# Rebuilding the head of an attention and MLP kernel: token-major scores by half supergroups, and two TensorE jobs handed to DMA

## The chip, the cores and the metric

One core of a Trainium2 chip. The metric is the device time of one execution in microseconds (us), and the median of several executions stands for a kernel. The time of an execution is about 1.8 us longer than the span of its trace. "Granted clock" is the share of full speed that TensorE's throttle granted; a run's mean of 0.994 stands for some 7 us at half speed (in after_again's trace, mean 0.994, the half speed lasts from 25.52 to 32.35 us, 6.83 us). All runs compared here are fast (a run counts as slow when it is over 1.5% above the fastest of its kernel), unless a text says otherwise.

## The reference, cut to what matters

```python
def mab(q, kv):                       # attention, one head, 128 channels
    s = scale * (q @ kv.T)
    a = softmax(s)
    return a @ kv
for b in range(4):                    # batches of N = 12480 tokens
    h = mab(inducing, x[b])           # 32 inducing rows read all tokens of x
    attn = mab(x[b], h)               # the tokens read the 32 rows back
    g = attn @ w_in                   # 128 -> 2048
    g = max(g, 0) + alpha * min(g, 0)
    out[b] = g @ w_out                # 2048 -> 128
```

The first `mab` is a reduction over all tokens of a batch: nothing of the second can start before the last token of x was read. For batches 1 to 3 the kernel hides it under the work of the batch before. For batch 0 nothing is there to hide it under: that is the **head**. The rest is the **body**.

## The kernel before

Tokens come in supergroups of 2048 (six, plus a rest of 192), and a supergroup has four groups (q = 0 to 3). In the body a step is four "ring fills" (matmuls of the attention weights with `hW` into four PSUM banks), their eviction through relu by ScalarE and VectorE, and sixteen output matmuls; a group has four steps. (`hW` is h times `w_in`. The activation is computed as (1 - alpha) relu(g) + alpha g: relu's part goes through `W1`, which is `w_out` scaled by 1 - alpha, and the linear part through one 128x128 matrix A = `w_in` (alpha `w_out`). The "alpha copies" are the small instructions that bring alpha into place for this.) The attention weights stand in SBUF four times over ("replicas"), so that four matmuls run side by side in the array (the first four fills all start between 28.47 and 28.48 us).

The head of before, with cuts:

```python
    def a_xpose_pe(st, u):                      # x of supergroup u to channel-major
        for i in range(2):
            ...                                 # 8 transposes into one bank, then a copy
    def a_scores(st, u, by_dma=True):
        for q in range(NQ):                     # 32 rows x 512 tokens, four at once
            mm(ps[32 * q : 32 * q + 32, :], IT[:], st.xT[:, u, q, :])
        ...                                     # exp, with the sums by accum_out
    def e_xpose_pe(st, u): ...                  # exp back to token-major: 4 transposes, a copy
    def a_accum(st, u, into=None, first=False): ...   # pooling: 16 matmuls
    ...
    for i in range(n - 1):
        a_xpose_pe(st, order[i + 1])
        if i > 0:
            e_xpose_pe(st, order[i - 1])
        a_scores(st, order[i], by_dma=False)
        if 0 < i < n - 2:
            a_accum(st, order[i - 1], pool, i == 1)
    ...
    h_den(st)                                   # 1 / softmax sum, folded into `fr`
    w_inT(0)                                    # half of w_in transposed by TensorE
    a_accum(st, order[n - 1], pool)
    pin(nc.vector.tensor_copy(out=st.hacc[:], in_=pool))
    warm(6)                                     # filler transposes, results unused
    h_transpose(st)
    warm(6)
    b_scores_pe(st, 0, 0)                       # replicas of group 0: scores + exp
    h_weights(st, first=True)                   # hW
    warm(8)
    # the body; tasks that ride in its first groups:
    for q in range(1, NQ):
        at(0, lambda q=q: b_scores_pe(st, 0, q), q, (240, "A", 480))
    at(0, lambda: w_inT(KC // 2), 3, (460, "A", 960))
    ...                                         # four sets of denominators, A = w_in W
```

The softmax here doesn't subtract the row's maximum and nothing guards it: scores larger than these inputs give would overflow.

Of the kernel before, what the change touches and what calls it, by code (L numbers as in the profile page):

```python
# [24 lines left out]
def kernel(  # L25
# [49 lines left out]
    gt_pool = ctx.enter_context(tc.tile_pool(name="gtp", bufs=4))  # L75
    rep_pool = ctx.enter_context(tc.tile_pool(name="repp", bufs=3))
# [23 lines left out]
    def new_batch(b):  # L100
        st = Batch()
        st.b = b
        st.xT = xt_pool.tile([C, NS, NQ, GRP], bf16, name="xT", tag="xT")
        st.xTr = xt_pool.tile([C, JR, PR], bf16, name="xTr", tag="xTr")
        st.xn = {}
        st.e1 = {}
        st.e1T = {}
        st.es = work.tile([P, NS + 1], f32, name="es", tag="es")
        st.hacc = work.tile([P, C], f32, name="hacc", tag="hacc")
        st.e2 = {}  # L110
        st.d = {}
        st.rep = {}
        st.rden = {}
        nc.vector.memset(st.es[:], 0.0)
        nc.vector.memset(st.hacc[:], 0.0)
        return st
# [32 lines left out]
    def a_xpose_pe(st, u):  # L149
        xn = st.xn[u]  # L150
        if u < NS:
            for i in range(2):
                tp = bank()[:].bitcast(bf16)
                for k in range(2 * NB):
                    q, j = 2 * i + k // NB, k % NB
                    pin(nc.tensor.transpose(
                        tp[:, k * P : (k + 1) * P], xn[:, q, j * C : (j + 1) * C], ident[:]
                    ))
                dst = st.xT[:, u, 2 * i : 2 * i + 2, :].rearrange("c q t -> c (q t)")
                if i == 0 or u == order[-1]:  # L160
                    pin(nc.vector.tensor_copy(out=dst, in_=tp))
                else:
                    pin(nc.scalar.copy(out=dst, in_=tp))
        else:
            tp = bank()[:].bitcast(bf16)
            for j in range(JR):
                pin(nc.tensor.transpose(
                    tp[:, j * PR : (j + 1) * PR], xn[:, j, :], ident[:PR, :PR]
                ))
            pin(nc.vector.tensor_copy(  # L170
                out=st.xTr[:].rearrange("c j p -> c (j p)"), in_=tp[:, :REM]
            ))

    def e_xpose_pe(st, u):
        e1 = st.e1.pop(u)
        tp = bank()[:].bitcast(bf16)
        if u < NS:
            e1T = work.tile([P, NB, P], bf16, name="e1T", tag="e1T")
            for j in range(NB):
                pin(nc.tensor.transpose(  # L180
                    tp[:, j * P : (j + 1) * P], e1[:, j * P : (j + 1) * P], ident[:]
                ))
            pin(nc.vector.tensor_copy(
                out=e1T[:].rearrange("p j m -> p (j m)"), in_=tp[:, : NB * P]
            ))
        else:
            e1T = work.tile([P, JR, M], bf16, name="e1Tr", tag="e1Tr")
            for j in range(JR):
                pin(nc.tensor.transpose(
                    tp[:PR, j * M : (j + 1) * M], e1[:, j, :PR], ident[:M, :M]  # L190
                ))
            pin(nc.vector.tensor_copy(
                out=e1T[:PR].rearrange("p j m -> p (j m)"), in_=tp[:PR, : JR * M]
            ))
        st.e1T[u] = e1T

    def a_scores(st, u, by_dma=True):
        ps = bank()
        if u < NS:
# [6 lines left out]
            if by_dma:  # L206
                e1T = work.tile([P, NB, P], bf16, name="e1T", tag="e1T")
                pin(nc.sync.dma_start_transpose(out=e1T[:], in_=e1[:]))
        else:
            mm(ps[0:M, :REM], IT[:], st.xTr[:].rearrange("c j p -> c (j p)"))  # L210
            e1 = e1r
            pin(nc.scalar.activation(
                out=e1[:, :, :PR],
# [3 lines left out]
            if by_dma:  # L217
                e1T = work.tile([P, JR, M], bf16, name="e1Tr", tag="e1Tr")
                pin(nc.sync.dma_start_transpose(
                    out=e1T[:], in_=e1[:].rearrange("m j p -> m (j p)")  # L220
                ))
        if by_dma:
            st.e1T[u] = e1T
        else:
            st.e1[u] = e1



    def a_accum(st, u, into=None, first=False):
        xn = st.xn.pop(u)  # L230
        e1T = st.e1T.pop(u)
        alone = into is None
        ps = bank() if alone else into
        if u < NS:
            for j in range(NB):
                for q in range(NQ):
# [4 lines left out]
                        start=(j == 0 and (alone or first)), stop=(j == NB - 1),  # L241
                        skip_group_check=not alone,
                    )
            if alone:
                pin(nc.vector.tensor_tensor(
                    out=st.hacc[:], in0=ps[:, :C], in1=st.hacc[:], op=ADD
                ))
        else:
            for j in range(JR):
                mm(  # L250
                    ps[0:M, :C], e1T[:PR, j, :], xn[:, j, :],
                    start=(j == 0 and alone), stop=(j == JR - 1),
                    skip_group_check=not alone,
                )
            if alone:
                pin(nc.vector.tensor_tensor(
                    out=st.hacc[0:M, :], in0=ps[0:M, :C], in1=st.hacc[0:M, :], op=ADD
                ))
# [22 lines left out]
    def h_weights(st, first=False):  # L281
# [8 lines left out]
        for j0, j1 in ((0, 1), (1, NJ)) if first else ((0, NJ),):  # L290
            pin(nc.vector.tensor_copy(
                out=st.hW[:, j0:j1, :].rearrange("m j k -> m (j k)"),
                in_=ps[:, j0 * P : j1 * P],
            ))

    def h_linear(st):
# [3 lines left out]
        pin(nc.vector.tensor_copy(out=st.hA[:], in_=pa[:, :C]))  # L300


    def b_scores(st, s):
        ps = bank()
        if s < NS:
# [3 lines left out]
            pin(nc.scalar.activation(out=e2[:], in_=ps[:], func=EXP, scale=scale))  # L309
            w = GRP  # L310
        else:
            mm(ps[0:M, :REM], st.hT, st.xTr[:].rearrange("c j p -> c (j p)"))
            e2 = work.tile([M, REM], bf16, name="e2r", tag="e2r")
            pin(nc.scalar.activation(out=e2[:], in_=ps[0:M, :REM], func=EXP, scale=scale))
# [7 lines left out]
    def b_rep(st, s):  # L322
# [3 lines left out]
        for r in range(4):  # L326
            pin(nc.sync.dma_start(out=rep[32 * r : 32 * r + 32], in_=dv))
        for q in range(nq):
# [3 lines left out]
    def b_scores_pe(st, s, q):  # L332
        if q == 0:
            st.rep0 = rep_pool.tile([P, NQ, GRP], bf16, name="rep", tag="rep")
        ps = bank()
        mm(ps[:], st.hT4[:], st.xT[:, s, q, :])
        pin(nc.scalar.activation(out=st.rep0[:, q, :], in_=ps[:], func=EXP, scale=scale))
        st.rep[s * NQ + q] = st.rep0[:, q, :]

    def b_den_pe(st, s, q):  # L340
        if q == 0:
            st.rden[s] = work.tile([P, NB, NQ], f32, name="rd", tag="rd")
        e2 = st.rep[s * NQ + q] if q else st.rep0[:, 0, :]
        ps = bank()
        for j in range(NB):
            mm(ps[:, j : j + 1], e2[:, j * P : (j + 1) * P], pick[:, 0:1])
        pin(nc.vector.reciprocal(
            out=st.rden[s][:, :, q : q + 1].rearrange("p j q -> p (j q)"), in_=ps[:, :NB]
        ))

# [134 lines left out]
    make_identity(nc, ident32[:])  # L485
    al_f = const.tile([KC, P], f32, name="al_f")
    nc.sync.dma_start(out=al_f[:], in_=moe_alpha.rearrange("(k p) -> k p", p=P))
    for u in order[3:]:
# [4 lines left out]
    pin(nc.gpsimd.dma_start(  # L493
        out=w_out_f[:], in_=moe_w_out.rearrange("(k p) c -> p k c", p=P)
    ))
# [5 lines left out]
    for q in range(4):  # L501
# [16 lines left out]
    alp = bank()  # L518
    alT = const.tile([P, KC], f32, name="alT")
    nc.tensor.transpose(alp[:, :KC], al_f[:], ident32[:KC, :KC])  # L520
    nc.vector.tensor_copy(out=alT[:], in_=alp[:, :KC])
    om_al = const.tile([P, KC], f32, name="om_al")
    nc.vector.tensor_scalar(
        out=om_al[:], in0=alT[:], scalar1=-1.0, scalar2=1.0, op0=MULT, op1=ADD
    )
# [4 lines left out]


# [9 lines left out]
    def warm(n):  # L541
        tp = accs[1][:].rearrange("p k c -> p (k c)").bitcast(bf16)
        for k in range(n):
            pin(nc.tensor.transpose(tp[:, k * P : (k + 1) * P], ident[:], ident[:]))

    def w_inT(k0):
        wtp = bank()[:].bitcast(bf16)
        for k in range(8):
            pin(nc.tensor.transpose(
                wtp[:, k * P : (k + 1) * P],  # L550
                w_in_b[:, (k0 + k) * P : (k0 + k + 1) * P], ident[:],
            ))
        pin(nc.scalar.copy(
            out=winT[:, k0 : k0 + 8, :].rearrange("p k c -> p (k c)"), in_=wtp
        ))
# [16 lines left out]
    pool = accs[0][:, 0, :]  # L572
    n = len(order)
    a_xpose_pe(st, order[0])
    for i in range(n - 1):
        a_xpose_pe(st, order[i + 1])
        if i > 0:
            e_xpose_pe(st, order[i - 1])
        a_scores(st, order[i], by_dma=False)
        if 0 < i < n - 2:  # L580
            a_accum(st, order[i - 1], pool, i == 1)
    a_scores(st, order[n - 1], by_dma=False)
    e_xpose_pe(st, order[n - 2])
    a_accum(st, order[n - 3], pool)
    h_sum(st)
    w_scale(W1, om_al)
    w_scale(AW, alT)
    e_xpose_pe(st, order[n - 1])
    a_accum(st, order[n - 2], pool)
    h_den(st)  # L590
    w_inT(0)
    a_accum(st, order[n - 1], pool)
    pin(nc.vector.tensor_copy(out=st.hacc[:], in_=pool))
    warm(6)
    h_transpose(st)
    warm(6)
    b_scores_pe(st, 0, 0)
    h_weights(st, first=True)
    warm(8)
# [15 lines left out]
    for q in range(1, NQ):  # L615
# [156 lines left out]
```

## Time and profile before

597.37 us, median of 3 runs (596.58 to 597.43). The trace below is of another, slower execution: its span of 597.17 us stands for a time of some 598.9 us (an estimate, with the 1.8 us of above).

| reading | us | view |
|---|---|---|
| last piece of x landed / w_in / w_out | 19.87 / 23.12 / 26.34 | landings of DMAs in the trace |
| last half's transposes begin | 21.38 | timeline |
| first ring fill | 28.47 | timeline |
| group 1's first fill | 35.20 | timeline |
| first output matmul of group 5 | 61.62 | timeline |
| end | 597.17 | trace |

From the page of before (busy times; then busy tenths in 40 slices of the span, and the granted clock in the same slices):

```profile
...
PE 582.9 (98%) x9186; PEld 435.0 (73%) x9186; DVE 518.6 (87%) x878; ACT 507.1 (85%) x994; POOL 84.9 (14%) x170
...
PE   4999999999999999999999999999999999999997
...
PEclk9999999999999999999999999999999999999999
...
```

TensorE is busy 98% of the span. Of the forty slices (14.9 us each) only the first and the last show less than nine tenths, and the body begins at 28.47 us: what a change of the head can win lies in these first 30 us.

From the timeline of before (start, duration, engine, line, instruction, count; in brackets the idle time before it and what ended it):

```profile
...
20.92 0.62 PE L156 MATMUL ring_85<-ident,xn 128*128 128x128 bf16 x8
...
21.38 0.61 PE L156 MATMUL ring_86<-ident,xn 128*128 128x128 bf16 x8
...
26.39 0.49 PE L94 MATMUL ring_82<-fr,hacc 128*128 128x128 f32 x2
...
27.26 0.39 PE L94 MATMUL ring_83<-xT,hT_494 128*128 128x512 bf16 x1
...
28.47 0.39 PE L94 MATMUL ring_85<-rep,hW 32*128 32x512 bf16 x1
...
30.24 1.05 PE L94 MATMUL acc_87<-W_168,gt 128*128 128x128 bf16 x16
...
35.20 0.38 PE L94 MATMUL ring_82<-rep,hW 32*128 32x512 bf16 x1
...
```

After the last transposes come scores, exp and pooling, then the transpose of the pooled rows (26.39), the replica's scores (27.26) and the first fill (28.47). Between them stand waits for copies and exps of the other engines, in part filled with the filler transposes: a chain, in which each piece stands behind the one before it.

### The profile page before, as it was taken

The page shows a single profiled execution, that of the slowest core. Times are in us where ns is not written, and L with a number is a line of the kernel's source. Part 1 is how long each engine was busy: PE and PEld are TensorE (multiplying, and loading weights), DVE is VectorE, ACT ScalarE, POOL GpSimd, SP SyncE. Part 2 cuts the span into 40 slices and gives each one's busy share as a digit, 9 for nine tenths or more (in the row PEclk, how much of TensorE's full clock was granted, in tenths as well). Part 3 has the DMA queues.
Part 4 walks back from the last instruction along what each step waited for, and adds up shares of the span by engine and source line. Part 5 has one row for each costly group of instructions (what it writes and reads, how often), then busy time and mean ns, then how long its engine had stood idle before and what let it go on. Part 6 is the DMA issues. An engine that isn't in the chain of part 4 may idle for free.

```text
span 597.2 us, 21700 instructions
## 1 busy us (share of the span) xinstructions
PE 582.9 (98%) x9186; PEld 435.0 (73%) x9186; DVE 518.6 (87%) x878; ACT 507.1 (85%) x994; POOL 84.9 (14%) x170
## 2 busy tenths in 40 slices
PE   4999999999999999999999999999999999999997
PEld 3677777777777777677777777777777777777775
DVE  2588899889889998899998989988988898998995
ACT  3588888898889888888888988889888889989886
POOL 6331111010111111101011111101011101101100
PEclk9999999999999999999999999999999999999999
DMA  9644799862237669983134478986212221221211
GB/s 197 161 93 103 162 161 176 172 105 85 68 87 147 134 141 173 166 154 112 40 99 120 101 162 157 173 177 103 86 68 80 80 98 57 83 97 56 93 46 61
DMA packets 79009, 69.18 MB, mean 116 GB/s; under 512 B 53200, under 2 KB 68448, under 8 KB 78912
## 3 DMA queue, kind: packets, MB, share of 16 engines
q0 software_dynamic: 12720, 39.30, 26.4%
q1 hardware_dynamic: 66048, 27.97, 24.2%
q8 instruction: 72, 1.18, 0.9%
q10 hardware_dynamic: 144, 0.52, 0.3%
q14 instruction: 25, 0.20, 0.1%
HBM read 39.94 MB, written 28.62 MB: 115 GB/s over the span
## 4 chain that ended last, share of the span: by engine, by line
PE 58%; ACT 0%; DVE 0%; issue 0%
PE acc_88 L94 21%; PE acc_87 L94 21%; PE ring_85 L94 3%; PE ring_83 L94 3%; PE ring_84 L94 3%; PE ring_82 L94 3%; PE ring_81 L94 3%; PE ring_86 L94 3%; ACT gt L405 0%; DVE gt L407 0%; DVE ob L456 0%
## 5 line engine op out<-in xcount | busy, mean ns | idle before, releaser
L94 PEld LDWEIGHTS <-gt 128*128 128x128 bf16 x6272 | 352.4, 98 | 78.9 <-issue 75.9
L94 PE MATMUL acc_87<-W_168,gt 128*128 128x128 bf16 (+1 forms) x3136 | 209.0, 220 | 0.0
L94 PE MATMUL acc_88<-W_168,gt 128*128 128x128 bf16 (+1 forms) x3136 | 208.8, 220 | 0.0
L465 POOL DMA_DIRECT2D out_dram<-ob x99 | 53.7, 542 | 492.8 <-DVE ob L456 422.3
L405 ACT ACTIVATE gt<-ring_83 128x512 bf16<-128x512 f32 (+1 forms) x160 | 95.5, 597 | 10.9 <-ACT gt L405 5.4
L405 ACT ACTIVATE gt<-ring_81 128x512 bf16<-128x512 f32 (+1 forms) x159 | 95.0, 597 | 11.2 <-PE ring_84 L94 5.6
L94 PE MATMUL ring_82<-rep,hW 32*128 32x512 bf16 (+1 forms) x270 | 101.6, 379 | 0.0
L94 PE MATMUL ring_83<-rep,hW 32*128 32x512 bf16 (+1 forms) x270 | 101.1, 378 | 0.0
L94 PE MATMUL ring_85<-rep,hW 32*128 32x512 bf16 (+1 forms) x267 | 100.4, 379 | 0.3 <-ACT gt L405 0.3
L94 PE MATMUL ring_84<-rep,hW 32*128 32x512 bf16 (+1 forms) x266 | 99.6, 378 | 0.8 <-DVE gt L407 0.8
L94 PE MATMUL ring_86<-rep,hW 32*128 32x512 bf16 (+1 forms) x264 | 99.3, 379 | 0.0
L94 PE MATMUL ring_81<-rep,hW 32*128 32x512 bf16 (+1 forms) x263 | 98.9, 379 | 0.0
L405 ACT ACTIVATE gt<-ring_84 128x512 bf16<-128x512 f32 x147 | 88.2, 600 | 12.0 <-ACT gt L405 5.4
L405 ACT ACTIVATE gt<-ring_85 128x512 bf16<-128x512 f32 (+1 forms) x147 | 87.7, 596 | 11.8 <-PE ring_82 L94 5.3
L405 ACT ACTIVATE gt<-ring_86 128x512 bf16<-128x512 f32 (+1 forms) x143 | 85.6, 599 | 12.3 <-ACT gt L405 5.9
L405 ACT ACTIVATE gt<-ring_82 128x512 bf16<-128x512 f32 (+1 forms) x142 | 84.9, 598 | 12.1 <-PE ring_85 L94 4.4
L407 DVE TENSOR_SCALAR gt<-ring_82 128x512 bf16<-128x512 f32 (+1 forms) x123 | 84.2, 684 | 8.5 <-PE ring_84 L94 4.1
L407 DVE TENSOR_SCALAR gt<-ring_86 128x512 bf16<-128x512 f32 (+1 forms) x116 | 79.4, 684 | 12.9 <-PE ring_82 L94 8.4
L407 DVE TENSOR_SCALAR gt<-ring_84 128x512 bf16<-128x512 f32 (+1 forms) x113 | 77.1, 682 | 9.3 <-PE ring_85 L94 3.8
L407 DVE TENSOR_SCALAR gt<-ring_85 128x512 bf16<-128x512 f32 x115 | 78.9, 686 | 7.1 <-PE ring_81 L94 2.5
L407 DVE TENSOR_SCALAR gt<-ring_83 128x512 bf16<-128x512 f32 x104 | 71.4, 687 | 9.4 <-PE ring_85 L94 4.4
L407 DVE TENSOR_SCALAR gt<-ring_81 128x512 bf16<-128x512 f32 x99 | 68.0, 687 | 6.8 <-PE ring_82 L94 2.3
(321 smaller groups left out, 372.1 us busy)
## 6 DMA issues: line engine op xcount, KB each, us to landing
out_dram<-ob POOLq DMA_DIRECT2D x96, 256.0 KB, 2.8
rep<-e2d SPq DMA_DIRECT2D x92, 128.0 KB, 3.0
xn<-in_x_dram POOLq DMA_DIRECT2D x18, 512.0 KB, 6.2
xn<-in_x_dram POOLq DMA_DIRECT2D x10, 256.0 KB, 8.9
w_out_f<-in_moe_w_out_dram POOLq DMA_DIRECT2D x1, 1024.0 KB, 13.9
xs<-in_x_dram ACTq DMA_DIRECT2D x1, 512.0 KB, 4.0
xs<-in_x_dram SPq DMA_DIRECT2D x1, 512.0 KB, 5.0
w_in_b<-in_moe_w_in_dram POOLq DMA_DIRECT2D x1, 512.0 KB, 11.9
```

What stands on the lines that cost most here:

```text
L94: return pin(nc.tensor.matmul(o, lhsT, rhs, start=start, stop=stop, **kw))
L405: pin(nc.scalar.activation(out=gt[:, r, :w], in_=ps[:, :w], func=RELU))
L407: pin(nc.vector.tensor_relu(gt[:, r, :w], ps[:, :w]))
L465: pin((nc.sync if last_one else nc.gpsimd).dma_start(out=dst, in_=ob[:pp, :nb, :]))
```

## The change: its intent and its diff

The head is to be shorter by a shorter chain, and TensorE is to be freed of three jobs in the first groups: the scores for the replicas of groups 1 to 3, half of the transposes of w_in (the other half stood in the head), and three of four sets of denominators (with all four groups' exps in one tile, one set of matmuls does). The first two go to DMA.

1. Scores are made token-major (x as the weights, the 32 inducing rows as the moving side), so that exp comes out as pooling needs it: no transposes of exp.
2. Pooling has x as the weights and exp as the moving side, so that its result is already transposed; no copy and transpose of the pooled rows.
3. The softmax sum is not divided out of h. Its reciprocal is applied as the scale of the second exp and in the eviction of `hW`.
4. All of it goes by half supergroups.
5. Replicas of groups 1 to 3 come by DMA through DRAM, as for all later supergroups; w_in is transposed by DMA; w_out is loaded in pieces, the one that is needed first ahead. The filler transposes go.

```diff
+    def p_scores(st, u, i):
+        for k, (xt, _) in enumerate(blocks):            # 8 blocks of 128 tokens
+            mm(ps[:pp, k * M : (k + 1) * M], xt, IT[:])
+        ...                                             # one exp, 128x256
+    def p_pool(st, u, i, first=False, last=False):
+        for k in range(0, nb, step):
+            mm(den[: step * M, :], e1t[...], ones[:pp, :], ...)      # sums
+        for k, (_, xk) in enumerate(blocks):
+            mm(pool, xk, e1t[:pp, k, :], ...)                        # 128 x 32
...
-    def b_scores_pe(st, s, q):
+    def b_scores_pe(st):                                # group 0 alone
...
-    def warm(n): ...
-    def w_inT(k0): ...                                  # 8 transposes, a ScalarE copy
+    def w_inT():
+        for k in range(0, KC, KC // 2):
+            pin(nc.sync.dma_start_transpose(
+                out=winT[:, k : k + KC // 2, :], in_=w_in_b[:, k * P : (k + KC // 2) * P]
+            ))
...
+    p_xpose(st, *halves[0])
+    for i in range(n):
+        if i + 1 < n:
+            p_xpose(st, *halves[i + 1], last=i + 2 == n)
+        p_scores(st, *halves[i])
+        if i > 0:
+            p_pool(st, *halves[i - 1], first=i == 1)
+        if i == 3:
+            alphas()
+            w_scale(W1, om_al)
+            w_scale(AW, alT)
+    p_pool(st, *halves[n - 1], last=True)
+    et = p_sums(st)
+    p_h(st)
+    p_scale(st, et)
+    b_scores_pe(st)
+    h_weights(st, first=True)
+    b_scores(st, 0)
+    b_rep(st, 0, 1)                                     # replicas of groups 1 to 3 by DMA
+    w_inT()
...
-    for q in range(1, NQ):
-        at(0, lambda q=q: b_scores_pe(st, 0, q), q, (240, "A", 480))
-    at(0, lambda: w_inT(KC // 2), 3, (460, "A", 960))
-    ...                                                 # four sets of denominators
+    at(0, lambda: b_den(st, 0), 2, (130, "D", 250))     # one set
```

## The prediction

> **What bounds the kernel.** TensorE: the page gives it 98% busy of 597.2 us. That is the body, from the first ring fill (timeline: 28.47 us) to the end, where its waits on others sum to about 2 us (view of waits). A step of the body (four fills, sixteen output matmuls) recurs every 1.43 us. The change leaves the body's work alone, so only the head and the first two groups can pay: at most some 5%.
>
> **The head before.** Pieces of x land every 1.25 us, the last at 19.87, w_in at 23.12, w_out at 26.34 (landings in the trace). From the last transposes (20.92) to the first fill are 7.5 us of serial tail: copies, scores, exp, transposed exp, accumulate, denominator, pooled copy, transpose, exp, hW.
>
> **The head after.** A half needs 8 transposes (54 ns apart, 0.46 us), 8 score, 2 sum and 8 pooling matmuls. The last 18 have few columns but full 128x128 weights; the trace's 128x128 weights with one column start 24 to 29 ns apart[...]. Estimate: 1.0 us a half, under the 1.25 us of data, so the end of the loop is set by the last landing. The start is 0.9 us earlier, since the cast of x no longer stands behind the alpha copies. Early transposes are 105 ns apart until 14.4 us; I expect that again, and a lag of 0.5 to 1 us at the last piece.
> Tail: last transposes end near 21.0; cut copies 0.7, scores 0.25, exp 0.5, pooling 0.4, pooled copy 0.5, scores 0.4, exp 0.7 with semaphores. First fill near 25.2: **3.2 us earlier**.
>
> **The first two groups.** Removed from TensorE: three replica scores (0.23 each), eight w_in transposes (0.46), three of four denominator sets (0.35): about 1.5 us; from ScalarE three exps and a 1.0 us copy. Added: a wait. The e2 write takes 1.7 us undisturbed (4.6 in traffic), the four replica DMAs 4.0 together; from an exp ending at 25.7 they are there at 31.5 to 32.5. Group 1 wants them four steps after the first fill, about 30.8. So TensorE stalls 0.7 to 1.7 us and gives back most of the 1.5. w_in by DMA transpose (5 to 7 us for 16 blocks) lands near 35, about when A wants it; stall 0 to 0.5. W1's first stripe is scaled by 25.2, the rest by 29.6: no wait.
>
> **Sum.** -3.2 -1.5 +1.1 = -3.6: **593.8 us** (0.6% less), 8 in 10 between 591.3 and 596.7. Faster by over 2%: 1%; within 2%: 98%; slower: 1%.
>
> **Signs.** Right: first ring fill at 24.4 to 26; score and pooling matmuls 24 to 30 ns apart when warm; last transposes within 1.5 us of the last landing; a gap of TensorE before group 1's first fill of 0.5 to 2 us, ended by the replica DMA; from first fill to end within 1 us of before's 568.7. Wrong: score matmuls 55 ns apart (then TensorE, at 1.5 us a half, paces the head); a slow TensorE through the tail because the warm-up transposes are gone[...].
>
> **What would make it wrong.** Replicas or transposed w_in later than 33 and 37 us (traffic), each us of which is a us of the result; a cold array after 21 us; a wait for W1 if w_out's strided pieces land late. In the other direction: no lag at the last piece and quiet DMA, 2 us more gain.

Its readings are from the trace of before. There transposes start 107 ns apart up to 13.6 us and 56 ns apart from 14.8 on, and the clock's records begin, with full speed, at 14.53; this is what "warm" means, and "cold" the opposite. The writes of exp (128 KB) took 1.7 to 5.6 us, the four replica DMAs (128 KB each) 4.0 to 9.8 from the first issue to the last landing, and the DMA transposes of sixteen blocks 4.7 to 8.1.

## The result and the profile after

593.5 us, median of 4 runs (592.68 to 595.19), against 597.4 (596.58 to 597.45). (Before has one execution more here than above.) The ratio is 0.9936, 95% interval 0.9917 to 0.9956: faster beyond doubt, by 0.6%.

The page after, same lines as before:

```profile
...
PE 577.6 (98%) x9209; PEld 433.4 (73%) x9209; DVE 517.9 (88%) x869; ACT 501.7 (85%) x986; POOL 87.8 (15%) x174
...
PE   5899999999999999999999999999999999999997
...
PEclk9999999999999999999999999999999999999999
...
```

The timeline after, in two windows (the first ends at 24 us):

```profile
...
20.20 0.62 PE L171 MATMUL ring<-ident,xn 128*128 128x128 bf16 x8 [0.18 <-DMA xn<-in_x_dram]
...
20.85 0.59 ACT L179 COPY xT<-ring 128x512 bf16<-128x512 bf16 x1 [0.60 <-PE ring L171]
...
22.36 0.35 PE L95 MATMUL acc<-e1t,xn 128*128 128x32 bf16 x8
...
22.75 0.29 DVE L238 CAST hT<-acc 128x128 bf16<-128x128 f32 x1
...
23.10 0.39 PE L95 MATMUL ring<-xT,hT 128*128 128x512 bf16 x1
...
23.52 0.69 ACT L380 ACTIVATE rep<-ring,rs 128x512 bf16<-128x512 f32 x1 [1.28 <-PE ring L95]
...
```

```profile
...
24.28 1.64 PE L95 MATMUL ring<-rep,hW 32*128 32x512 bf16 x8 [0.25 <-DVE hW L247]
...
25.85 1.07 PE L95 MATMUL acc<-W,gt 128*128 128x128 bf16 x16
...
30.33 0.39 PE L95 MATMUL ring<-rep,hW 32*128 32x512 bf16 x3
...
30.90 0.09 PEld L95 LDWEIGHTS <-hW 32*128 32x128 bf16 x1 [0.47 <-DMA rep<-e2d]
30.90 0.38 PE L95 MATMUL ring<-rep,hW 32*128 32x512 bf16 x1 [0.18 <-DMA rep<-e2d]
...
```

The tail has become: last transposes 20.20, the cut copy (20.85), two exps, the last pooling (22.36), the pooled copy (22.75), scores (23.10), exp (23.52), first fill 24.28. That is 4.2 us earlier than before. At 30.90 the fourth fill of group 1 waits 0.47 us for a replica's DMA (by the weight load's idle time; the matmul itself, whose ends are modelled, shows 0.18).

The chain of waits of the changed kernel in its first 45 us (start, duration, what; each piece was released by the one before it):

```profile
...
10.27 9.88 DMA xn<-in_x_dram
20.15 0.05 issue
20.20 0.63 PE ring L171 x8
...
24.82 2.06 DMA e2d<-e
...
28.49 2.37 DMA rep<-e2d
...
30.90 0.38 PE ring L95
...
```

The chain runs through the loads of x up to 20.15 and TensorE picks the last piece up 0.05 us later. It then leaves the engines once more, for the write of exp and the replicas' return (24.82 to 30.85).

Since the order of instructions is fixed, two traces can be laid on each other by the start of a group's first output matmul (counted by 64 output matmuls a group; since the rest of a batch has only 32, "group 34" and "group 38" here lie half a group in):

| us | before | after | difference |
|---|---|---|---|
| first ring fill | 28.47 | 24.28 | -4.19 |
| group 5, first output matmul | 61.62 | 56.69 | -4.94 |
| group 34 | 228.54 | 223.60 | -4.94 |
| group 38 | 253.04 | 247.09 | -5.95 |
| end | 597.17 | 591.08 | -6.09 |

From group 5 to group 34, 167 us, the distance of the two kernels stays at -4.94, with one step at -5.01. So up to there the change acts before group 5 and nowhere else, as it was meant to; behind group 36 the distance drifts by some tenths. But the spans differ by 6.1 us, the medians of the times by 3.9. The difference between these two numbers, 2.2 us, lies in the choice of the traces: that of before is of an execution of some 598.9 us, 1.5 above its median, that of the changed kernel of one of 592.84, 0.7 below. What moves single executions so much is the subject of the experiments.

### The profile page after: what moved, and what is told of

Its sections match the earlier page's. It is cut to its first block, busy times and chain, and to the rows that moved or that the text cites. A ratio compares the mean times of both kernels' runs of the same rounds, so it can differ in the third digit from the quotient of the medians.

```text
span 591.1 us, 21747 instructions
## 1 busy us (share of the span) xinstructions
PE 577.6 (98%) x9209; PEld 433.4 (73%) x9209; DVE 517.9 (88%) x869; ACT 501.7 (85%) x986; POOL 87.8 (15%) x174
## 3 DMA queue, kind: packets, MB, share of 16 engines
q8 instruction: 72, 1.18, 0.8%
## 4 chain that ended last, share of the span: by engine, by line
PE 94%; DMA 4%; ACT 1%; issue 0%; DVE 0%; SPq 0%; POOL 0%; ACTq 0%; POOLq 0%
PE acc L95 67%; PE ring L95 27%; DMA xn<-in_x_dram 3%; DMA rep<-e2d 0%; ACT gt L439 0%; DMA e2d<-e 0%; SPq L371 0%; DVE ob L490 0%; DVE gt L441 0%; ACT rep L380 0%; POOL xnr L133 0%; PE ring L171 0%; ACT xT L179 0%; ACT e L353 0%; ACT e1t L196 0%
## 5 line engine op out<-in xcount | busy, mean ns | idle before, releaser
L439 ACT ACTIVATE gt<-ring 128x512 bf16<-128x512 f32 x899 | 469.5, 598 | 69.1 <-ACT gt L439 27.7
L441 DVE TENSOR_SCALAR gt<-ring 128x512 bf16<-128x512 f32 x669 | 435.1, 686 | 53.0 <-PE ring L95 38.6
L95 PE MATMUL acc<-W,gt 128*128 128x128 bf16 x6272 | 417.8, 220 | 0.5 <-POOL W L576 0.3
L95 PE MATMUL ring<-rep,hW 32*128 32x512 bf16 (+1 forms) x1600 | 158.1, 379 | 0.7 <-DVE hW L247 0.2
L95 PEld LDWEIGHTS <-hW 32*128 32x128 bf16 x1600 | 41.2, 91 | 42.8 <-DVE hW L247 1.2
L490 DVE TENSOR_TENSOR ob<-acc,rd 128x512 f32<-128x512 f32 x96 | 65.4, 682 | 2.5 <-PE acc L95 2.5
L95 PE MATMUL acc<-hA,rep 32*128 32x128 bf16 x392 | 19.8, 214 | 0.0
L95 PEld LDWEIGHTS <-rep 32*128 32x128 bf16 x392 | 15.6, 93 | 5.5
L128 POOL DMA_DIRECT2D xn<-in_x_dram x28 | 15.4, 555 | 2.5 <-DMA xn<-in_x_dram 2.4
L353 ACT ACTIVATE e<-ring 128x512 bf16<-128x512 f32 x18 | 11.0, 609 | 0.0
L261 ACT ACTIVATE e<-ring 128x512 bf16<-128x512 f32 x18 | 10.9, 603 | 0.0
```

What stands on the lines that cost most here:

```text
L95: return pin(nc.tensor.matmul(o, lhsT, rhs, start=start, stop=stop, **kw))
L128: pin(nc.gpsimd.dma_start(out=xn[:, i * w : (i + 1) * w, :], in_=src[:, i * w : (i + 1) * w, :]))
L261: pin(nc.scalar.activation(out=e1[:], in_=ps[:], func=EXP, scale=scale, accum_out=st.es[:, u : u + 1]))
L353: pin(nc.scalar.activation(out=e2[:], in_=ps[:], func=EXP, scale=scale_of(st)))
L439: pin(nc.scalar.activation(out=gt[:, r, :w], in_=ps[:, :w], func=RELU))
L441: pin(nc.vector.tensor_relu(gt[:, r, :w], ps[:, :w]))
```

## The experiments

Ratios are to the kernel before, run on the same chip in the same rounds. "Fill to group 5" is the time from the first ring fill to the first output matmul of group 5; "landing" is that of the last piece of x. The last three columns are from one trace each. Clocks are listed of all runs, the slow ones of after_late and best included.

| label | median us | ratio, 95% interval | runs with clock 0.997 or less | landing | first fill | fill to group 5 |
|---|---|---|---|---|---|---|
| before | 597.4 | 1 | 0 of 33 (later rounds) | 19.87 | 28.47 | 33.16 |
| after | 593.5 | 0.9936 [0.9917, 0.9956] | 1 of 4 | 20.15 | 24.28 | 32.41 |
| before_again | 597.41 | 0.9989 [0.9975, 1.0004] | 0 of 4 | 19.64 | 28.32 | 33.16 |
| after_again | 594.26 | 0.9940 [0.9923, 0.9956] | 5 of 6 | 20.59 | 24.72 | 34.16 |
| both_pe | 597.02 | 0.9990 [0.9970, 1.0010] | 6 of 6 | 20.98 | 25.11 | 35.69 |
| whole_sg | 594.22 | 0.9936 [0.9916, 0.9956] | 2 of 4 | 19.89 | 24.50 | 32.04 |
| before_nowarm | 598.25 | 1.0017 [1.0005, 1.0029] | 3 of 5 | 20.70 | 27.69 | 35.94 |
| after_warm_m | 594.51 | 0.9953 [0.9939, 0.9968] | 1 of 6 | 20.09 | 24.40 | 32.89 |
| after_warm_t | 594.13 | 0.9942 [0.9930, 0.9955] | 1 of 6 | 20.58 | 24.89 | 32.23 |
| both_pe_warm | 595.96 | 0.9981 [0.9969, 0.9993] | 1 of 5 | 20.94 | 25.18 | 34.35 |
| win_pe_warm | 593.95 | 0.9939 [0.9925, 0.9952] | 0 of 6 | 20.56 | 24.87 | 33.22 |
| alpha_first | 594.42 | 0.9940 [0.9927, 0.9953] | 2 of 4 | 19.97 | 24.10 | 34.27 |
| after_late | 606.3 (603.6 of the four fast) | 1.0092 [1.0056, 1.0127] | 6 of 6 | 20.43 | 24.78 | 33.51 |
| best | 597.62 (597.56 of the six fast) | 0.9992 [0.9971, 1.0013] | 3 of 7 | 20.97 | 25.28 | 39.79 |

### The two kernels once more

No edit: second traces.

> The kernel before, unchanged, for a second trace. Theory 1 (the 1.0 us by which the body differs at groups 34 to 38 is chance: one late replica DMA in the trace of before): first ring fill again at 28.5 us and the first output matmul of group 5 at 61.6, both within 0.3 us, but the 1.1 us wait for a replica DMA is absent or lies in another group. Theory 2 (it belongs to the kernel's order of DMAs): the same wait of about 1 us in the same group. Time 597.4 within 1 us.

> The changed kernel, unchanged. Its four times spread over 2.5 us (592.7 to 595.2), those of before over 0.9. Theory 1 (the spread comes from single waits for a DMA in the body or for the replicas of group 1): the trace shows the first ring fill within 0.3 us of 24.3 and any difference of span sits in one or two waits for a replica DMA. Theory 2 (the head now ends with the last landing of x, so that every delay of the loads goes through to the end): first ring fill moves by 0.5 us or more together with the last landing of x (20.15 in the first trace). Time 592.5 to 595, ratio to before 0.991 to 0.996.

Before: 597.41 us. The second trace runs 0.14 us ahead of the first from group 0 to group 34 and 1.37 us ahead at group 38: the first had one wait there, the second has no wait for a replica in the body. That is theory 1. Here is that wait, from the timeline of TensorE's weight loads in the first trace of before:

```profile
...
241.10 0.10 PEld L94 LDWEIGHTS <-hW 32*128 32x128 bf16 x3
242.34 0.09 PEld L94 LDWEIGHTS <-hW 32*128 32x128 bf16 x1 [1.14 <-DMA rep<-e2d]
...
```

One replica's DMA came 1.14 us late, in one trace. So the step from -4.94 to -5.95 in the table above is no gain of the change. With the span of the second trace (595.59 us) the traces differ by 4.5 us.

The changed kernel: 594.26 us, and a trace with a span of 594.84 us, 3.8 longer than the first. Three things are in it. The landing of x is 0.44 us later, and the first fill is 0.44 us later with it: theory 2, but just under the 0.5 us that it asked for. TensorE waits once for a replica, which is theory 1; from the timeline of its weight loads:

```profile
...
97.02 0.10 PEld L95 LDWEIGHTS <-hW 32*128 32x128 bf16 x3
98.59 0.09 PEld L95 LDWEIGHTS <-hW 32*128 32x128 bf16 x1 [1.47 <-DMA rep<-e2d]
...
```

And a third that neither theory had. From the view of windows (per stretch: length, busy time of each engine with its instructions, granted clock, DMA share, GB/s), first of the changed kernel's first trace, then of its second:

```profile
...
24.00:28.00 4.00, 3.23 (x42) 1.83 (x39) 3.89 (x8) 3.49 (x8) 2.46 (x3) 1.00 0.28 80
28.00:32.00 4.00, 3.82 (x56) 2.64 (x54) 3.30 (x7) 3.10 (x6) 4.00 (x5) 1.00 0.73 172
...
```

```profile
...
24.00:28.00 4.00, 3.50 (x31) 1.83 (x24) 3.36 (x6) 3.21 (x6) 2.35 (x3) 0.69 0.25 76
28.00:32.00 4.00, 4.00 (x38) 2.29 (x37) 1.95 (x4) 1.65 (x4) 4.00 (x5) 0.50 0.61 149
...
```

The clock (third number from the end) is 1.00 throughout in the first trace; in the second it is 0.69 and 0.50. The clock's records put the half speed at 25.52 to 32.35 us (mean 0.994, 6.83 us). In these 8 us TensorE issued 69 instructions in place of 98. From fill to group 5 it took 34.16 us in place of 32.41: this costs 1.75 us.

The prediction named this ("a slow TensorE through the tail because the warm-up transposes are gone") among the signs of its being wrong, but did not count it. In the ten runs of the changed kernel's own rounds, six had a mean clock of 0.997 or less.

### Half the head, and its order

both_pe is the changed kernel with replicas, denominators and w_in done by TensorE as before (all sixteen transposes of w_in now ride in groups 0 and 1; before had eight of them in its head):

```diff
-    b_scores_pe(st)
+    b_scores_pe(st, 0, 0)
     h_weights(st, first=True)
-    b_scores(st, 0)
-    b_rep(st, 0, 1)
-    w_inT()
...
-    at(0, lambda: b_den(st, 0), 2, (130, "D", 250))
+    for q in range(1, NQ):
+        at(0, lambda q=q: b_scores_pe(st, 0, q), q, (240, "A", 480))
+    ...                                   # four sets of denominators, as before
+    at(0, lambda: w_inT(0), 3, (460, "A", 960))
+    at(1, lambda: w_inT(KC // 2), 0, (460, "A", 960))
```

> The new head, but the first group's replicas, denominators and the transposes of w_in by TensorE as before. Theory A (the rebuilt head is nearly the whole gain): first ring fill 24.0 to 24.4, first output matmul of group 5 some 0.3 to 1.0 us later than the changed kernel's 56.7, time 0.3 to 1.0 us above it, no wait for a replica DMA in group 1. Theory B (moving the work to DMA pays for the 1.5 us of TensorE that it takes away): group 5 at 58.0 or later, time 1.3 to 1.8 us above. Theory C (the wait for the replicas eats more than it saves): group 5 at 56.5 or earlier, time the same or less.

597.02 us: the whole gain is gone, more than any of the three theories had. But all six runs had a low clock, and so had its trace. The first fill came at 25.11, outside the expected 24.0 to 24.4, because x landed late (20.98); its distance from the landing is 4.13 us, as in the changed kernel. Two causes stand together, so it was made again with fillers (below).

whole_sg walks the head by whole supergroups (for it the pool of exp tiles grows from three buffers to six, and the alpha copies move to `i == 2`):

```diff
-    for i in range(n):
-        if i + 1 < n:
-            p_xpose(st, *halves[i + 1], last=i + 2 == n)
-        p_scores(st, *halves[i])
-        if i > 0:
-            p_pool(st, *halves[i - 1], first=i == 1)
+    for i in range(n):                    # over whole supergroups
+        if i + 1 < n:
+            for h in wholes[i + 1]:
+                p_xpose(st, *h, last=h == halves[-1])
+        for h in wholes[i]:
+            p_scores(st, *h)
+        if i > 0:
+            for h in wholes[i - 1]:
+                p_pool(st, *h, first=h == halves[0])
```

> The changed kernel with its head walked by whole supergroups in place of halves: same instructions, but both halves' transposes, then both halves' scores, then both halves' pooling. Theory A (the halves pay because the tail after the last landing is shorter): last transposes start at the same 20.2 us, first ring fill 0.4 to 1.0 us later (one more half's scores and pooling, about 0.5 us, stand behind the last landing). Rival (the halves do not matter, since the other half is worked on while the last piece's copies and exp run): within 0.2 us of 24.3. Time follows the first fill.

From its timeline, TensorE alone:

```profile
...
19.94 0.62 PE L171 MATMUL ring<-ident,xn 128*128 128x128 bf16 x8 [0.37 <-DMA xn<-in_x_dram]
...
22.46 0.20 PE L95 MATMUL acc<-ones,e1t 128*128 128x1 bf16 x2
...
24.50 0.39 PE L95 MATMUL ring<-rep,hW 32*128 32x512 bf16 x4 [0.30 <-DVE hW L247]
```

The last transposes start as soon as the piece lands (19.89), and the first fill comes 4.61 us after the landing; in the changed kernel's head it is 4.13, in four traces (after, after_again, both_pe, alpha_first). The halves are worth 0.48 us of the tail, as theory A had it, if one counts from the landing; by the clock the first fill is only 0.22 us later, since x landed 0.26 earlier. The time does not show it: 594.22 us, the same as the changed kernel, and group 1's first output matmul starts at 32.41 against 32.54. Two waits make up for it: the changed kernel's trace has 0.25 us for a stripe of W1 at 27.69, which whole_sg's has not, and at group 1 it waits 0.47 us for a replica (landed at 30.85) where whole_sg waits 0.36 (30.71). So in these two traces the 0.48 us are lost again before group 1's output.

### The clock

before_nowarm deletes the fillers from before, three lines:

```diff
-    warm(6)
     h_transpose(st)
-    warm(6)
     b_scores_pe(st, 0, 0)
     h_weights(st, first=True)
-    warm(8)
```

> The kernel before with its twenty filler transposes between the head's last matmuls deleted, nothing else. So far the granted clock's mean is 0.998 or more in every run of before, and 0.997 or less in 6 of 10 runs of the changed kernel, whose second trace shows the clock at half from 25.52 to 32.35 us. Theory 1 (the fillers kept TensorE busy enough; without them the clock drops in the tail of the head in some executions): half or more of the runs at 0.997 or less, these 1 to 2.5 us longer than the others. Rival (the clock drops for another reason, such as the small score and pooling matmuls of the new head): all runs at 0.998 or more, time within 0.5 us of before's or slightly less.

598.25 us against 597.43 in the same rounds, ratio 1.0017, and three of five runs at 0.994 to 0.997. All 37 runs of before with its fillers have 0.998 or more. So losing the fillers is enough to bring the drop, without the new head's small matmuls. From the view of windows of before_nowarm, the two stretches on either side of the drop:

```profile
...
25.03:28.45 3.42, 2.17 (x29) 0.78 (x22) 1.85 (x7) 1.92 (x3) 2.25 (x3) 1.00 0.01 2
28.45:31.86 3.41, 3.19 (x25) 1.98 (x22) 2.21 (x4) 2.21 (x5) 3.41 (x4) 0.50 0.00 0
...
```

The half speed (0.50 in the second stretch) lies behind the first fill (27.69); in the 3.42 us before it, which hold the end of the tail, TensorE was busy 2.17 us. From fill to group 5 it took 35.94 us against 33.16. The fillers themselves cost little: from the last transpose to the first fill 6.54 us without and 6.70 with them.

One half of the expectation failed: the three runs with a low clock (598.06 to 599.76) are not 1 to 2.5 us longer than the two others (597.75, 598.79). The landing of x and single waits for a replica move a run by as much, and five runs cannot separate them.

after_warm_m and after_warm_t put 22 fillers into the idle places of the changed kernel's tail and first two steps, as matmuls and as transposes (the diff shows the matmuls):

```diff
+    def warm(n, ring_bank=False):
+        tp = bank()[:] if ring_bank else accs[1][:].rearrange("p k c -> p (k c)")
+        for k in range(n):
+            mm(tp[:, (k % NB) * P : (k % NB + 1) * P], ident[:], ident[:], skip_group_check=True)
...
+    warm(3, ring_bank=True)
     p_pool(st, *halves[n - 1], last=True)
+    warm(3, ring_bank=True)
     et = p_sums(st)
     p_h(st)
     p_scale(st, et)
+    warm(2)
     b_scores_pe(st)
     h_weights(st, first=True)
     b_scores(st, 0)
+    warm(6)
...
+    at(0, lambda: warm(4), 0)
+    at(0, lambda: warm(4), 1)
```

> The changed kernel with 22 filler matmuls (128x128 identity by itself) in the idle places of TensorE from the last pooling to the second step of group 0. Theory 1: no run under 0.998, first ring fill within 0.3 us of 24.3, median 592.5 to 593.3 against 594.3 of the changed kernel, and a smaller spread. Rival (the clock is not what spreads the runs): still half of the runs at 0.997 or less, or all at 1.0 and the same median. If the fillers stand in the way: all clocks full, but the first fill 0.5 us or more later.

> The same places and number of fillers, but transposes as in the kernel before in place of matmuls. [...]the clock drops as often as without fillers (half of the runs at 0.997 or less); if transposes count as matmuls do, no run is under 0.998 and the time equals that of the matmul fillers within 0.3 us.

(The last text puts two outcomes against each other.)

The clock held in most runs: one run in six at 0.997 with either kind, so that transposes did as well as matmuls here, and the one that has a trace had its half-speed stretch at 97.37 us, where TensorE waited 2.07 us for a replica, not in the head. From the view of windows of after_warm_m, the stretch that contains the first fill:

```profile
...
24.27:27.69 3.42, 3.40 (x47) 1.99 (x45) 3.08 (x7) 2.72 (x6) 2.14 (x3) 1.00 0.23 72
...
```

Over the four kernels with fillers and an untouched body it is 3 of 23; over the five versions of the new head without (after, after_again, both_pe, whole_sg, alpha_first) 16 of 24. The means alone do not tell where in a run the clock fell; that is known for the traced runs only.

The time did not follow: 594.51 and 594.13 us against 594.26. The fillers put the first fill 4.31 us after the landing in place of 4.13, and both traces have waits of 1.2 to 2.1 us for a replica at 97 us, as after_again had. So the expectation of 592.5 to 593.3 was wrong: the clock is one part of the spread and holding it did not show in the median of six runs.

### What moving work to DMA is worth, at a full clock

both_pe_warm is both_pe with `warm(3)`, `warm(3)`, `warm(2)`, `warm(8)`, `warm(4)`, `warm(4)` in the same places. win_pe_warm is after_warm_m with the transposes of w_in alone on TensorE:

```diff
-    w_inT()
...
+    at(0, lambda: w_inT(0), 3, (460, "A", 960))
+    at(1, lambda: w_inT(KC // 2), 0, (460, "A", 960))
```

> The new head with the first group's replicas, denominators and the transposes of w_in by TensorE, and the filler matmuls. Its version without fillers had all six runs at 0.993 to 0.997 and 597.0 us, which mixes the clock with the cost of the work itself. With a full clock: Theory A (the rebuilt head is nearly the whole gain, the DMA replicas a wash): 593.0 to 594.0. Theory B (taking replicas and transposes off TensorE and ScalarE is worth 1.5 us or more): 594.5 to 596. First ring fill 24.0 to 24.5 in both.

> New head, DMA replicas, filler matmuls, but w_in transposed by TensorE and copied by ScalarE in groups 0 and 1. From first ring fill to the first output matmul of group 5 it took 32.9 us with both by DMA and 34.35 with both by TensorE (full clock in both). If the two parts share the 1.5 us by TensorE's work (0.9 for sixteen transposes, 1.1 for replicas and denominators): 33.5 to 33.8. If ScalarE's two copies of 1.0 us count more than TensorE's work: 34.0 or more. If the wait for the replicas hides the transposes of w_in, which then run in it: 32.9 to 33.2.

Fill to group 5, all with a full clock in the stretch: 32.89 us with both jobs by DMA (after_warm_m), 33.22 with w_in by TensorE (nearest to the last of its three expectations, 32.9 to 33.2), 34.35 with both by TensorE. So with these traces the two jobs together (replicas with their denominators, and w_in) are worth 1.46 us. The medians say the same: 595.96 less 594.51 is 1.45 us. Theory B holds for both_pe and for both_pe_warm, whose first fill (25.18, landing 20.94) missed the expected 24.0 to 24.5. The split into 1.13 us for the replicas and 0.33 for w_in is not settled: one trace each cannot carry it, since after_warm_t, with both jobs by DMA as in after_warm_m, took 32.23, and the waits for replicas in these stretches differ (0.9 us in after_warm_m, 0.4 in after_warm_t, 0.2 in win_pe_warm). Measured against after_warm_t, the DMA transposes of w_in would be worth 0.99. With the 0.9 us of wait taken out of the 32.89, the gross saving is some 2.4 us, more than the 2.0 of TensorE's own work for these jobs (0.9 and 1.1 in the expectation). A likely reason is read from ScalarE's timeline of both_pe_warm, not shown by a run of its own: its exps of replicas and its copy of w_in stand between the evictions that the fills wait for.

```profile
...
27.53 0.71 ACT L381 ACTIVATE rep<-ring,rs 128x512 bf16<-128x512 f32 x1
...
29.52 0.69 ACT L381 ACTIVATE rep<-ring,rs 128x512 bf16<-128x512 f32 x1
...
30.58 0.69 ACT L381 ACTIVATE rep<-ring,rs 128x512 bf16<-128x512 f32 x1
31.15 1.02 ACT L605 COPY winT<-ring 128x1024 bf16<-128x1024 bf16 x1
...
```

With w_in by TensorE the median is 593.95 us and the ratio 0.9939, not distinguishable from the changed kernel's. With fillers in place, this part of the change could be left out.

Of the 2.9 us between before and after_warm_m in the same rounds (597.43 and 594.51), half is thus the moved jobs; the new head with all jobs on TensorE gains 1.5 (597.43 less 595.96), although its first fill is 3.3 us earlier, in part, it seems, because sixteen transposes of w_in stand behind it where before had eight.

### The start of the head

alpha_first puts the alpha copies back in front of the cast of x:

```diff
+    alphas()
     xn0 = xn_pool.tile([P, NQ, GRP], bf16, name="xn", tag="xn")
...
         if i == 3:
-            alphas()
```

> The changed kernel with the alpha copies put back before the cast of x, as in the kernel before; the first transposes then start about 1.1 us later (7.8 in place of 6.7). The prediction counted an earlier start of 0.9 us. Theory (the head's end is set by the last landing of x, so the start has slack): distance from the last landing of x to the first ring fill still 4.1 to 4.3 us. Rival (TensorE still lags behind the data): 4.6 us or more.

```profile
...
7.82 1.89 PE L171 MATMUL ring<-ident,xn 128*128 128x128 bf16 x16 [1.07 <-DVE xn L599]
...
24.10 0.94 PE L95 MATMUL ring<-rep,hW 32*128 32x512 bf16 x6 [0.25 <-DVE hW L247]
```

The first transposes start at 7.82 in place of 6.70, and the first fill is 4.13 us after the landing (19.97), to the hundredth what it is in the changed kernel. The start has slack; the earlier start of 0.9 us that the prediction named was worth nothing at the first fill.

### An attempt at something better

Replica DMAs came late in the body when they were issued just behind a load of x. In after_again a load of 512 KB was issued at 89.42 and a replica's DMA at 89.56; the load landed at 96.78 and the replica at 98.55, 9.0 us after its issue. The replica issued 1.3 us earlier took 3.6. This does not hold for each: in the changed kernel's first trace a load was issued at 33.62, and of the replicas behind it the first (33.79) took 2.8 us and the next three 6.4 to 6.7. after_late moves the loads:

```diff
-                at(k, lambda n=n, u=u: a_load(states[n], u))
+                at(k + 1, lambda n=n, u=u: a_load(states[n], u))
```

> The changed kernel with each later batch's loads of x put one group later, so that a load is issued one output store later than now. In the traces the fourth replica DMA of a supergroup lands 6 us late when its issue falls just behind a load of x (second trace of the changed kernel: load issued at 89.42, replica at 89.56, landed 98.55, TensorE waits 1.47 us at 98.59). Theory (these single waits are the part of the spread that the clock does not explain): no wait for a replica DMA over 0.5 us after group 2 in the trace, and runs with a clock of 0.999 or more all within 0.7 us of each other, near 592.7. Rival (the waits move to other places, or the loads then come too late): such waits are still there, or waits for the transposed x appear, and runs with a full clock spread over 2 us again.

606.3 us, the worst of all. Two of its six runs are slow; the four others have a median of 603.6 (600.68 to 606.56), and the ratio is of these. TensorE's waits in its trace:

```profile
...
PEld L95 <- DMA xT<-xn: 8.6, 9, 2.0
...
```

The waits for replicas are gone from the body, as the theory had it. In their place are nine for the transposed x: the transposes are issued from the same queue, which now stands waiting for the load in front of them. From the waits of that queue, first in the changed kernel, then in after_late:

```profile
...
SPq L142 <- DMA xn<-in_x_dram: 3.3, 1, 3.3
...
```

```profile
...
SPq L142 <- DMA xn<-in_x_dram: 17.9, 3, 8.3
...
```

3.3 us have become 17.9. The rival had foreseen it.

best has the later loads, the matmul fillers, group 1's replica by TensorE and w_out in four stripes:

```diff
+    for j in range(NJ):
+        pin(nc.gpsimd.dma_start(out=w_out_g[:, :, j, :], in_=w_out_v[:, :, j, :]))
...
-    b_rep(st, 0, 1)
+    b_rep(st, 0, 2)
...
+    at(0, lambda: b_scores_pe(st, 1), 1, (240, "A", 690))
```

> The changed kernel with the later loads, the filler matmuls, the replica of group 1 by TensorE like that of group 0 (DMA brings only groups 2 and 3), and w_out loaded by four stripes in the order in which they are scaled. Expected: clock 0.999 or more in five of six runs, no wait for a replica in group 1, first output matmul of group 5 no more than 32.0 us after the first ring fill (32.4 in the changed kernel, 32.9 with fillers alone), median 592.0 to 593.0. If the extra exp of group 1 costs ScalarE what the wait cost TensorE: 32.4 to 33 us and 593 to 594.

597.62 us; its trace is slow (610.0 us), so it tells of mechanisms only. From its waits:

```profile
...
PEld L95 <- DMA xT<-xn: 9.7, 7, 5.2
PEld L95 <- DMA winT<-w_in_b: 5.6, 1, 5.6
...
```

The second half of the transposed w_in was issued at 32.13, a load of x at 32.50, and it landed at 40.48 where in the changed kernel it landed at 33.58. TensorE waited 5.6 us for it. No wait for a replica in group 1 was left, as expected; the expected median of 592.0 to 593.0 was missed by over 4 us, and four of seven runs, not five of six, had a clock of 0.999 or more. But since the later loads are in it and had cost some 9 us by themselves (603.6 against 594.3), the two small improvements remain untried by themselves. No version here beats the changed kernel beyond doubt.

## Why the prediction was right, point by point

The time was 593.5 us, 593.8 had been said. The direction and the two places of the gain were right. That the sum came so close is in part luck: two of its terms were too small, two costs were left out (the clock, and single late replicas in the body), and they nearly cancel.

1. **What bounds the kernel: right.** From group 5 to group 34 the distance of the two kernels stays within 0.07 us.
2. **The head, "3.2 us earlier": right in the main, too small.** It is 4.19 in the first trace. That trace has an early landing of x: in the four traces with this head and without fillers (after, after_again, both_pe, alpha_first) the first fill comes at 24.10 to 25.11, on average 3.8 us before that of before (28.32 and 28.47). "24.4 to 26" holds for nine of the eleven traces of the new head, not for the first. Score matmuls start 25 to 27 ns apart (in the first trace 27 before the clock was full and 25 after), and a half takes TensorE some 1.0 us while its data take 1.25. The lag that was allowed for, "0.5 to 1 us at the last piece", is 0.05 in all eleven traces, though the clock became full anywhere from 10.03 to 12.96 us (that is where its records begin: in the first trace at 10.06, and transposes start 107 ns apart before it and 56 behind it). The steps of the tail as written down add up to 3.45 us, which is what it took from the end of the last transposes (20.82) to the first fill (24.28); the prediction's 25.2 is 0.75 later than its own steps give from 21.0, and it does not say why. The earlier start had no effect (alpha_first).

   One part of the gain was overlooked, in the prediction and in the reading of the tail: in both traces of before the last transposes begin 1.5 and 1.6 us behind their data, so that 1.18 of the 4.19 us come before the tail and 3.01 within it. In before_nowarm, whose head is the same up to there, the clock was full at 11.38 us, not at 14.2 to 14.5, x landed 0.83 us later, and the lag was 0.05. How much of the lag belongs to the old head and how much to the moment at which the clock rises was not tested. Nor were the pieces of the new tail (token-major scores, pooling already transposed, the sum applied later) tried one by one; only the halves were (0.48 us).
3. **The first two groups, "-1.5 +1.1": right in sign, too small.** Fill to group 5 went from 33.16 to 32.41, -0.75 in place of -0.4. The wait was 0.47 us and not 0.7 to 1.7. Counted from the first fill, the replicas came when the prediction had them (6.57 us; 6.3 to 7.3 had been said), but group 1 wanted them later: its first fill came 6.05 us after the first of all, and not 5.6. With the same head, the jobs moved to DMA are worth 1.46 us net; before had half of the w_in transposes in its head and not in these groups, so that less was to be saved there.
4. **The clock: named as a danger, not counted.** Six of the ten runs had a mean clock of 0.997 or less. One of them has a trace: there the clock fell to half behind the tail of the head, and from fill to group 5 that cost 1.75 us. That it fell in the same place in the other five is not shown. The mean of the six is 594.8 us, that of the four others 593.7; these are few runs. So the clock explains a part of the distance between the -4.94 of the first two traces at group 5 and the -3.9 of the medians (-3.6 in the second rounds). The early landing of x in the first trace and late replicas in the body are other parts, and no run gives each its share.
5. **"From first fill to end within 1 us of before's 568.7": missed, both ways.** It was 566.8 in the first trace of the changed kernel and 570.1 in the second; 567.3 in the second of before. Single waits for a replica, 1 to 2 us each, and the clock decide it: between 566.8 and 570.1 lie 1.75 us of the clock and 1.56 of one replica.
6. **W1 and the transposed w_in: nearly right.** The view of waits has 0.3 us for W1, where no wait had been expected, and none for w_in.

What stays open: why a replica's DMA that is issued behind a load comes so late, and not every time; what lets the clock fall (TensorE was busy 2.17 us of the 3.42 before the drop in before_nowarm, 2.53 of 3.41 in both_pe and 2.78 of 3.41 in after_again, but 2.53 of 3.42 from 15.28 to 18.70 us in after_again, where no drop followed); and whether the full-clock runs of the changed kernel (592.7 to 595.2) spread by such waits alone. Such waits were seen in three traces (after_again, after_warm_m and after_warm_t, at 97 to 99 us), not in every run.

## What to carry to other kernels

When a head ends with the last byte of input, as here (0.05 us of lag), only the chain after the last landing counts: shorten that, and do not pay for an earlier start (in alpha_first transposes that start 1.12 us later leave the first fill 4.13 us behind the landing, where it is in the changed kernel). First see that the engine does keep up with its data: the head before stood 1.5 us behind them. Fillers that look like waste may be holding the clock up (here three of five runs had 0.997 or less without them, none of 37 with them); before they are deleted, look at the granted clock of several runs, since one trace may miss the drop (the first of the changed kernel shows 1.00 from 24 to 36 us, while six of ten runs had a mean of 0.997 or less). And lay two traces on each other by a counted instruction: it separates in a minute what the change did from what chance did. Then take a second trace of each, since one landing or one wait moves such a distance by 0.4 to 2 us.
